# Loading the remainder rows of w_k into both halves of the partitions and converting them where they stay

## The chip, the cores and the metric

The kernel runs on one core of a Trainium2 chip, in one launch. The metric is device time in microseconds (us): the median of three runs of the kernel before is 696.64 us (696.33 to 697.31). One of its executions was also taken by the profiler; all rows below are of that one.

## The reference

Three stages stand one behind the other, on 2 batches of 4160 tokens with 192 features:

```python
# 1. a causal convolution of 7 taps with weights of its own for each token and head
w = softmax(weight_gen)                                  # (2, 4160, 8, 7)
x = einsum('bshk,bskhg->bshg', w, windows_of_7(x))       # (2, 4160, 192)
# 2. a gated two-layer block on a mix of each token and the one before it
xk = mu_k * x + (1.0 - mu_k) * x_prev
xr = mu_r * x + (1.0 - mu_r) * x_prev
x = sigmoid(xr @ w_r) * (maximum(xk @ w_k, 0.0) ** 2 @ w_v)   # w_k (192, 1024)
# 3. a second block with a convolution of 3 taps along the tokens
h = maximum(x @ w_in, 0.0)
out = (h * sigmoid(conv3(h, conv_w))) @ w_out
```

`w_k` and the other weights come as 64-bit floats; the activations are 32-bit. The kernel rounds each weight to 32 bits itself, from the two 32-bit words of each number, and splits it into a high part that TensorE takes at full rate and a low part that holds the rest.

## The kernel before, in words

The tokens are cut into ten tiles (two of 238, seven of 476, one of 352) times two batches. For each tile, GpSimd (or VectorE for the first) multiplies the windows of `rows` by the softmax weights into `prod`; the seven taps are added up, by TensorE in the first tile, with the identity as weights; TensorE transposes the result (`tok`) so that features lie on the partitions; `mixing` makes `xk` and `xr`, again as a high and a low part, in `xA` (features 0 to 127) and `xB` (the remaining 64 features: the high part on one half of the partitions, the low part on the other). `moe1` multiplies these with `wkA` and `wkB`: five matmuls for each of eight blocks of 128 columns, three with `wkA`, then two with `wkB`, first with its high part, then with its low part. ScalarE squares, ScalarE and VectorE split the result into `s`, `out_passes` multiplies it with `wv`, and `moe2` does the like with `w_in`, the convolution and `w_out`.

Because `xB` holds high and low features on the two halves of the partitions, `wkB` needs the same 64 rows of `w_k` (rows 128 to 191) on both halves: `wkB[:, 0]` the high part, `wkB[:, 1]` the low part. How these rows get there is what the change touches.

A weight goes through `prepare` in chunks of up to 512 columns. Each chunk has a load (`fetch`, issued by SyncE into one of three slots of `stage`) and a conversion (`narrow`, then `split`). In mode 0, the mode of the first chunks, a conversion is one ScalarE activation from `stage` into a PSUM bank, two VectorE TENSOR_SCALARs and one SCALAR_TENSOR_TENSOR, two matmuls (with `ident` in full 32 bits, then with `signs`), a ScalarE CAST of the high part, a third matmul that takes it off again, and a ScalarE CAST of the low part. `MODES` gives the mode of each chunk in its order.

All engine instructions are first recorded in a list, and `Program.schedule` (lines 136 to 255) gives them their order: it estimates each instruction's time, walks the dependences forward and backward `ROUNDS` times, and emits each engine's instructions by the start times so found. So line 255 stands for nearly all instructions in the profile. `SLACK` adds time between an engine's result and its use by TensorE, `PACE` stretches the estimates for an engine, and 3.507 is the estimate of how late a load lands. These constants only set the order. On each engine the instructions then run in that order, each when its operands are there; two engines that write the same `prod` buffer wait for its reader.

Before the first real matmul, TensorE runs 26 matmuls on `signs` (lines 1078 to 1080).

Of the kernel before, what the change touches and what calls it, by code (L numbers as in the profile page):

```python
# [29 lines left out]
NF = DFF // 128  # L30
LAG = 12
WARM = 26
SLACK = {"ACT": 0.311, "DVE": 0.274, "POOL": 0.239}
PACE = {"ACT": 1.045, "DVE": 1.035, "POOL": 1.037}
ROUNDS = 13
HELD = [85.0, 140.0, 215.0, 290.0, 365.0, 440.0, 515.0]
HIGH = range(5)
LOWS = {(NTILE - 1, NB - 1, k) for k in range(6, NF)}
SUMS = {(1, 0, 1), (1, 1, 0), (1, 1, 1)}
MODES = [0, 0, 0, 0, 0, 0, 2, 2, 2, 2, 2, 0, 2, 2, 2, 2, 2]  # L40

S_LAG, G_LAG = 3.25, 4.75
S_LAG_HALF, HSTEP = 3.25, 1
# [6 lines left out]
def f(ap):  # L50
    return ap.bitcast(F32)


class Program:
# [81 lines left out]
    def schedule(self):  # L136
        n = len(self.ops)
# [70 lines left out]
        def forward(rank):  # L208
            nonlocal when
            when = hold[:]  # L210
            start, last, table = [0.0] * n, 0.0, ACTF.Exp
            wires = dict.fromkeys(self.real, 0.0)

            def step(i, eng, t):
                nonlocal last, table
                start[i] = t
                if turns[i] is not None:
                    t = t + (0.0 if turns[i] == table else 1.3)
                    table = turns[i]
                end = t + late[i]  # L220
                if load[i]:
                    wires[eng] = max(wires[eng], t + dur[i] + 0.55) + moved[i]
                    end = wires[eng] + 3.507
                last = max(last, end)
                for j in succ[i]:
                    when[j] = max(when[j], t + dur[i] if eng in ("PE", "POOL") and eng == name[j] else end + slack(i, name[j]))
                return t

            walk((pred, succ), lambda i: (rank[i], i), step)
            return start, last  # L230

        def backward(start, last):
            nonlocal when
            full = [dur[i] + 0.55 + moved[i] + 3.507 if load[i] else late[i] for i in range(n)]
            when = [full[i] - dur[i] for i in range(n)]
            rank = [0.0] * n

            def step(i, eng, t):
                rank[i] = last - t - dur[i]
                for j in pred[i]:  # L240
                    when[j] = max(when[j], t + dur[i] - dur[j] + (dur[j] if name[j] in ("PE", "POOL") and name[j] == eng else full[j] + slack(j, eng)))
                return t

            walk((succ, pred), lambda i: (-start[i], -i), step)
            return rank
# [24 lines left out]
def conv_moe_kernel(ctx: ExitStack, tc: tile.TileContext, xp, wg_first, wg_rest, w_k, w_v, w_r, w_in, conv_w, w_out, out):  # L270
# [40 lines left out]
    wkA = new("wkA", [128, 2, DFF], F32R)  # L311
# [92 lines left out]
    def fetch(w, parts, n):  # L404
        wide = w.dtype != F32
        st = {"wide": wide}
        if wide:
            st["raw"] = raw_r()
            dst, w = st["raw"], w.bitcast(U32)
            for p0, p1, c0, ap in parts(w, 2):  # L410
                SP.dma_start(out=dst[p0:p1, :, :].rearrange("p a b -> p (a b)")[:, c0:c0 + ap.shape[-1]] if len(ap.shape) == 2 or ap.shape[0] * ap.shape[1] == 128
                             else dst[p0:p1, 0:n, :].rearrange("p (a b) c -> p a (b c)", a=ap.shape[1]), in_=ap)
        else:
            st["x"] = f(raw_r().rearrange("p a b -> p (a b)"))
            for p0, p1, c0, ap in parts(w, 1):
                SP.dma_start(out=st["x"][p0:p1, c0:c0 + ap.shape[-1]] if len(ap.shape) == 2
                             else st["x"][p0:p1, 0:n].rearrange("p (a b) -> p a b", a=ap.shape[1]), in_=ap)
        return st
# [60 lines left out]
    def chunk_rem(src, B, twin):  # L479
        def go(x):  # L480
            y = wb_r()
            split(y[:, 0], y[:, 1], x)
            for part, a in ((0, 0), (64, 0), (0, 1), (64, 1)):
                SP.dma_start(out=f(B[part:part + 64, a]).rearrange("p (h c) -> p h c", h=2),
                             in_=f(y[:, a if part == 0 or twin else 0]))

        return lambda: fetch(src, lambda w, k: [(0, 128, 0, bass.AP(tensor=w.tensor, offset=w.offset + 128 * w.ap[0][0], ap=[[w.ap[0][0], 64], [512 * k, 2], [1, 512 * k]]))], 512), 512, go

    def chunk_in(src, A, c):
        sl = slice(512 * c, 512 * c + 512)  # L490
        return (lambda: fetch(src, lambda w, k: [(0, 128, 0, cols(w, k, 0, 128, 512 * c, 512))], 512), 512,
                lambda x: split(A[:, 0, sl], A[:, 1, sl], x))
# [515 lines left out]
    def before_first():  # L1008
        for a in att_r.tiles:
# [8 lines left out]
    attention(0, 1, -99.6, -83.7, 0.1, POOL)  # L1018
    softmax_load(1, wg_rest[:, :slots[1] * KH], -99.5)
    softmax(1, 0, slots[1], DVE, (-92, -91.9, -91.8, -91.7, -91.6, -91.5), am_r.tiles[0])  # L1020
    prepare((-99.75, -99.7, -99.4), [(-82, chunk_rem(w_k, wkB, True)), (-81, chunk_in(w_k, wkA, 0)),
                                     (-0.5, chunk_out(w_v, wv, 0)), (0.4, chunk_out(w_v, wv, 1)), (1.0, chunk_in(w_k, wkA, 1)),
                                     (1.4, chunk_out(w_v, wv, 2)), (2.4, chunk_out(w_v, wv, 3)), (3.4, chunk_r()),
                                     (6.0, chunk_rem(w_in, wiB, False)), (8.0, chunk_in(w_in, wiA, 0)), (10.0, chunk_out(w_out, wo, 0)),
                                     (10.4, chunk_conv()), (12.0, chunk_in(w_in, wiA, 1)), (14.0, chunk_out(w_out, wo, 1)),
# [122 lines left out]
```

## Time and profile before

| what | value |
|---|---|
| median of 3 runs | 696.64 us |
| the profiled execution's own time | 696.22 us |
| its span (first to last instruction) | 694.4 us |
| TensorE matmul busy (PE) | 683.8 us, 98% |
| TensorE weight load busy (PEld) | 603.0 us, 87% |
| VectorE busy (DVE) | 590.0 us, 85% |
| ScalarE busy (ACT) | 630.3 us, 91% |
| GpSimd busy (POOL) | 531.3 us, 77% |
| granted TensorE clock | full in all 40 slices |

The span is 1.8 us shorter than the execution's time; that is what lies before the first and after the last instruction. Shares over the whole span hide that the program has two regimes. In the first 100 us the weights are loaded and converted while the first tiles run; from then on the same tile work repeats. A busy matmul engine is not one at its peak, since matmuls overlap and their ends are modelled. `pa`, `pc`, `am`, `ar`, `bm` and `br` are PSUM banks; `bm` and `br` carry the conversions of the weights until they are needed as accumulators.

### The profile page before, as it was taken

What the parts mean: (1) busy time and instruction counts of PE and PEld (TensorE: products, weight loads), DVE (VectorE), ACT (ScalarE), POOL (GpSimd) and SP (SyncE); (2) the same over time, 40 slices, a digit from 0 to 9 for tenths busy, and PEclk for the clock granted to TensorE, in tenths of its full rate; (3) what the DMA queues carried; (4) which work ended last, traced back from release to release, by engine and by line L of the source; (5) the groups of instructions that cost most, each with busy time, mean ns of one, the idle gap of its engine ahead of it and who ended that gap; (6) DMA issues with size and microseconds to landing.
All of it is one profiled execution on the core that took longest, in us unless ns stands there. A gap on an engine that the chain in (4) does not pass through costs nothing.

```text
span 694.4 us, 10540 instructions
## 1 busy us (share of the span) xinstructions
PE 683.8 (98%) x3473; PEld 603.0 (87%) x3473; DVE 590.0 (85%) x1003; ACT 630.3 (91%) x1333; POOL 531.3 (77%) x388
## 2 busy tenths in 40 slices
PE   8999999999999999999999999999999999999997
PEld 7799887888888888888888888888888888899997
DVE  7999998889879888988798978988897768686787
ACT  4988999999999998999999899898999999999996
POOL 3899999996998799669976997599929996243335
PEclk9999999999999999999999999999999999999999
DMA  8886021222021310130212112121202000200010
GB/s 298 262 210 236 23 68 42 72 86 63 8 86 64 86 65 29 65 86 13 79 65 71 24 57 93 35 54 57 80 22 71 8 28 14 65 8 28 6 33 31
DMA packets 20790, 48.43 MB, mean 70 GB/s; under 512 B 3456, under 2 KB 16256, under 8 KB 20608
## 3 DMA queue, kind: packets, MB, share of 16 engines
q1 hardware_dynamic: 20592, 47.58, 23.2%
q8 instruction: 27, 0.44, 0.3%
q14 instruction: 27, 0.22, 0.1%
q10 hardware_dynamic: 144, 0.18, 0.1%
HBM read 27.40 MB, written 6.39 MB: 49 GB/s over the span
## 4 chain that ended last, share of the span: by engine, by line
PE 86%; DVE 7%; ACT 4%; issue 1%; DMA 1%; SPq 0%; DVEq 0%; ACTq 0%
PE pa L255 25%; PE pc L255 21%; PE bm L255 13%; PE am L255 12%; PE br L255 8%; PE ar L255 7%; DVE pc L255 2%; DMA sw<-in_rest_dram 1%; DVE stage L255 1%; DVE g L255 1%; DVE s L255 1%; ACT pc L255 1%; ACT pa L255 1%; DVE mk L255 0%; DVE ar L255 0%
## 5 line engine op out<-in xcount | busy, mean ns | idle before, releaser
L255 POOL TENSOR_TENSOR prod<-rows,sw 128x1344 f32<-128x1344 f32 x68 | 210.3, 3092 | 13.7 <-PE pa L255 11.1
L255 DVE SCALAR_TENSOR_TENSOR pc<-h,cw,pc 128x476 f32<-128x476 f32 (+1 forms) x276 | 193.7, 704 | 27.2 <-ACT pc L255 24.4
L255 ACT ACTIVATE pa<-pa 128x476 f32<-128x476 f32 (+2 forms) x280 | 151.8, 546 | 11.5 <-PE pa L255 9.0
L255 POOL TENSOR_TENSOR prod<-prod 128x576 f32<-128x576 f32 (+1 forms) x126 | 154.2, 1224 | 8.4
L255 PE MATMUL bm<-g,wo 128*128 128x476 f32 (+1 forms) x411 | 135.2, 376 | 0.4 <-ACT stage L255 0.4
L255 PE MATMUL am<-s,wv 128*128 128x476 f32 (+2 forms) x464 | 129.8, 357 | 0.0
L255 PE MATMUL pa<-xA,wkA 128*128 128x476 f32 (+2 forms) x438 | 112.0, 360 | 0.8 <-DVE s L255 0.8
L255 PE MATMUL pc<-x,wiA 128*128 128x478 f32 (+1 forms) x414 | 111.8, 375 | 0.4 <-ACT x L255 0.2
L255 DVE TENSOR_TENSOR s<-pa,s 128x476 fp32r<-128x476 f32 (+1 forms) x137 | 86.7, 634 | 19.5 <-ACT s L255 18.6
L255 PE MATMUL br<-g,wo 128*128 128x476 f32 (+1 forms) x274 | 100.6, 375 | 0.0
L255 PE MATMUL ar<-s,wv 128*128 128x476 f32 (+2 forms) x336 | 99.8, 350 | 0.0
L255 ACT ACTIVATE h<-pc 128x478 f32<-128x478 f32 (+1 forms) x138 | 78.4, 569 | 17.8 <-PE pc L255 16.6
L255 ACT ACTIVATE pc<-h,cw 128x476 f32<-128x476 f32 (+1 forms) x138 | 91.7, 665 | 0.8
L255 ACT ACTIVATE pc<-pc 128x476 f32<-128x476 f32 (+1 forms) x152 | 84.3, 555 | 8.3 <-DVE pc L255 4.5
L255 POOL TENSOR_TENSOR g<-stage,g 128x476 fp32r<-128x476 f32 (+1 forms) x41 | 47.5, 1160 | 56.0 <-ACT g L255 44.1
L255 PEld LDWEIGHTS pa<-xA,wkA 128*128 128x128 f32 x438 | 79.0, 188 | 12.2 <-DVE s L255 1.3
L255 PEld LDWEIGHTS am<-s,wv 128*128 128x128 f32 x464 | 81.0, 188 | 9.3
L255 PEld LDWEIGHTS pc<-x,wiA 128*128 128x128 f32 x414 | 76.3, 188 | 11.7 <-DVE g L255 1.0
L255 PEld LDWEIGHTS bm<-g,wo 128*128 128x128 f32 x411 | 76.5, 188 | 11.2 <-ACT stage L255 0.8
L255 PE MATMUL pa<-xB,wkB 128*128 128x476 f32 (+2 forms) x292 | 82.7, 359 | 0.0
L255 PE MATMUL pc<-x,wiB 128*128 128x478 f32 (+1 forms) x276 | 81.7, 376 | 0.0
L255 ACT CAST s<-pa 128x476 fp32r<-128x476 f32 (+1 forms) x137 | 76.4, 558 | 1.1
(170 smaller groups left out, 1177.5 us busy)
## 6 DMA issues: line engine op xcount, KB each, us to landing
rows<-in_x_dram SPq DMA_DIRECT2D x14, 960.0 KB, 4.9
xB<-rm SPq DMA_DIRECT2D x28, 119.0 KB, 2.2
rows<-in_x_dram SPq DMA_DIRECT2D x4, 768.0 KB, 6.3
xB<-mk SPq DMA_DIRECT2D x16, 119.0 KB, 2.3
rows<-in_x_dram SPq DMA_DIRECT2D x2, 864.0 KB, 5.5
r<-r SPq DMA_DIRECT2D x14, 119.0 KB, 2.2
x<-x SPq DMA_DIRECT2D x14, 119.0 KB, 2.2
out_dram<-stage SPq DMA_DIRECT2D x7, 238.0 KB, 2.0
```

The costliest lines, as they stand in the source:

```text
L255: getattr(self.real[eng], method)(*a, **k)
```

## The change

`chunk_rem` loaded the 64 remainder rows once, with their 1024 columns laid over 128 partitions as two blocks of 512, converted them once into `x2[1]` (`wb_r`) and copied high and low part to both halves of `wkB` with four DMAs. `chunk_both` loads 512 columns of these rows twice, once to each half of the partitions, and converts them with the output straight in `wkB`. It does this for each of the two blocks of columns, so `w_k` now has four chunks instead of three; `MODES` has one more entry, and the constants of the order have other values. The rows of `w_in` are still done by `chunk_rem`.

```diff
-SLACK = {"ACT": 0.311, "DVE": 0.274, "POOL": 0.239}
-PACE = {"ACT": 1.045, "DVE": 1.035, "POOL": 1.037}
-ROUNDS = 13
+SLACK = {"ACT": 0.274, "DVE": 0.242, "POOL": 0.427}
+PACE = {"ACT": 1.037, "DVE": 1.015, "POOL": 1.003}
+ROUNDS = 15
...
-MODES = [0, 0, 0, 0, 0, 0, 2, 2, 2, 2, 2, 0, 2, 2, 2, 2, 2]
+MODES = [0, 0, 0, 0, 0, 0, 0, 2, 2, 2, 2, 2, 0, 2, 2, 2, 2, 2]
...
-                    end = wires[eng] + 3.507
+                    end = wires[eng] + 3.307
...
+    def chunk_both(src, B, c, twin):
+        sl = slice(512 * c, 512 * c + 512)
+
+        def go(x):
+            if twin:
+                split(B[:, 0, sl], B[:, 1, sl], x)
+                return
...
+        return lambda: fetch(src, lambda w, k: [(64 * h, 64 * h + 64, 0, cols(w, k, 128, 192, 512 * c, 512)) for h in range(2)], 512), 512, go
...
-    prepare((-99.75, -99.7, -99.4), [(-82, chunk_rem(w_k, wkB, True)), (-81, chunk_in(w_k, wkA, 0)),
-                                     (-0.5, chunk_out(w_v, wv, 0)), (0.4, chunk_out(w_v, wv, 1)), (1.0, chunk_in(w_k, wkA, 1)),
+    prepare((-99.75, -99.7, -99.4), [(-82, chunk_both(w_k, wkB, 0, True)), (-81, chunk_in(w_k, wkA, 0)),
+                                     (-0.5, chunk_out(w_v, wv, 0)), (0.4, chunk_out(w_v, wv, 1)), (0.9, chunk_both(w_k, wkB, 1, True)), (1.0, chunk_in(w_k, wkA, 1)),
```

The order moves with it. SyncE's queue at the start of the program, before (`sw` are the softmax weights, `rows` the windows of the input, `stage` the slots of the weight loads):

```order
L255 DMA rows_80<-in_x_dram 128x1536
L255 DMA stage<-in_moe_w_k_dram 128x1024
L255 DMA rows_81<-in_x_dram 128x1536
L255 DMA stage<-in_moe_w_k_dram 128x1024
L255 DMA sw<-in_rest_dram 128x224
L255 DMA stage<-in_moe_w_v_dram 128x2x384
L255 DMA sw<-in_rest_dram 128x448
L255 DMA rows_80<-in_x_dram 128x1536
L255 DMA stage<-in_moe_w_v_dram 128x2x384
L255 DMA wkB<-x_1_74 64x2x512 x2
L255 DMA stage<-in_moe_w_k_dram 128x1024
L255 DMA wkB<-x_1_74 64x2x512 x2
```

The first remainder load stood behind the first `rows`. The same place now:

```order
L255 DMA stage<-in_moe_w_k_dram 64x1024 x2
L255 DMA rows_80<-in_x_dram 128x1536
L255 DMA stage<-in_moe_w_k_dram 128x1024
L255 DMA rows_81<-in_x_dram 128x1536
L255 DMA stage<-in_moe_w_v_dram 128x2x384
L255 DMA sw<-in_rest_dram 128x224
L255 DMA sw<-in_rest_dram 128x448
L255 DMA stage<-in_moe_w_v_dram 128x2x384
L255 DMA rows_80<-in_x_dram 128x1536
L255 DMA stage<-in_moe_w_k_dram 64x1024 x2
L255 DMA stage<-in_moe_w_k_dram 128x1024
```

The two half loads of the remainder stand ahead of the first `rows`, the second `rows_80` has moved behind a load of `w_v`, and the four `wkB` copies are gone.

VectorE after the first softmax (`prod` are the products of the first tile, `bm` and `br` hold the first two chunks of `w_k` that are being converted), before:

```order
L255 TENSOR_TENSOR sw<-sw,am 128x224
L255 TENSOR_TENSOR prod_82<-rows_80,sw 128x1344
L255 TENSOR_TENSOR prod_83<-rows_80,sw 128x1344
L255 TENSOR_SCALAR stage<-bm 128x512
L255 TENSOR_SCALAR pc_114<-stage 128x512
L255 TENSOR_REDUCE am<-sw 128x32
L255 SCALAR_TENSOR_TENSOR g_76<-stage,pc_114 128x512
L255 TENSOR_SCALAR stage<-br 128x512
```

And now:

```order
L255 TENSOR_TENSOR sw<-sw,am 128x224
L255 TENSOR_SCALAR stage<-bm 128x512
L255 TENSOR_SCALAR pc_114<-stage 128x512
L255 TENSOR_TENSOR prod_82<-rows_80,sw 128x1344
L255 SCALAR_TENSOR_TENSOR g_76<-stage,pc_114 128x512
L255 TENSOR_TENSOR prod_83<-rows_80,sw 128x1344
L255 TENSOR_SCALAR stage<-br 128x512
```

Two instructions of the first conversion stand ahead of the first product, and the third stands between the products.

## Rows read from the trace of the kernel before

**Rows 1.** The page's head and first part: busy us (share) xinstructions.

```profile
span 694.4 us, 10540 instructions
PE 683.8 (98%) x3473; PEld 603.0 (87%) x3473; DVE 590.0 (85%) x1003; ACT 630.3 (91%) x1333; POOL 531.3 (77%) x388
```

**Rows 2.** Stretches: length, busy us (instructions) by engine, clock, DMA share, GB/s.

```profile
7.60:22.30 14.70, 14.63 (x78) 12.47 (x79) 14.02 (x27) 10.00 (x30) 10.32 (x4) 1.00 1.02 296
22.30:30.00 7.70, 6.53 (x37) 5.03 (x37) 7.43 (x18) 6.63 (x19) 7.54 (x5) 1.00 0.90 319
40.00:60.00 20.00, 19.31 (x156) 18.38 (x154) 19.53 (x43) 17.65 (x45) 19.31 (x17) 1.00 0.79 193
60.00:100.00 40.00, 38.26 (x254) 34.09 (x253) 37.93 (x73) 35.40 (x79) 37.40 (x29) 1.00 0.30 104
200.00:300.00 100.00, 100.00 (x474) 86.89 (x473) 89.55 (x146) 94.34 (x194) 80.94 (x56) 1.00 0.18 55
```

**Rows 3.** The chain that ended last, from 10 to 26 us.

```profile
3.21 7.57 DMA sw<-in_rest_dram
...
24.21 0.60 DVE stage L255
...
24.95 1.10 PE bm L255 x2
```

**Rows 4.** VectorE in order of time: start, us, instruction, idle time before.

```profile
5.94 3.03 DVE L255 TENSOR_TENSOR prod<-rows,sw 128x1344 f32<-128x1344 f32 x2
8.88 0.68 DVE L255 TENSOR_SCALAR stage<-bm 128x512 uint32<-128x512 uint32 x1
9.60 0.69 DVE L255 TENSOR_SCALAR pc<-stage 128x512 uint32<-128x512 uint32 x1
10.80 0.57 DVE L255 TENSOR_REDUCE am<-sw 128x32 f32<-128x224 f32 x1 [0.51 <-DMA sw<-in_rest_dram]
11.29 0.68 DVE L255 SCALAR_TENSOR_TENSOR g<-stage,pc 128x512 fp32r<-128x512 uint32 x1
11.88 0.68 DVE L255 TENSOR_SCALAR stage<-br 128x512 uint32<-128x512 uint32 x1
```

**Rows 5.** ScalarE in order of time, the first conversion's activation.

```profile
7.33 0.64 ACT L255 ACTIVATE bm<-stage 128x512 f32<-128x512 f32 x1 [3.08 <-DMA stage<-in_moe_w_k_dram]
```

**Rows 6.** TensorE in order of time.

```profile
2.59 4.87 PE L1080 MATMUL ar<-signs 128*128 128x256 f32 x26 [2.59 <-ACT signs L255]
7.64 3.16 PE L255 MATMUL pa<-prod,ident 128*128 128x192 f32 x18 [0.19 <-DVE prod L255]
10.64 1.02 PE L255 MATMUL bm<-stage,ident 128*128 128x512 f32 x2
11.50 0.49 PE L255 MATMUL pa<-prod,ident 128*128 128x192 f32 x2
12.02 0.50 PE L255 MATMUL bm<-g,signs 128*128 128x512 f32 x1
12.36 1.46 PE L255 MATMUL pa<-prod,ident 128*128 128x192 f32 x8
...
22.35 0.58 PE L255 MATMUL pc<-xA,wkA 128*128 128x238 f32 x3
...
23.86 0.45 PE L255 MATMUL br<-g,signs 128*128 128x384 f32 x1 [0.53 <-DVE g L255]
24.14 0.27 PE L255 MATMUL pc<-xB,wkB 128*128 128x238 f32 x1
24.95 1.10 PE L255 MATMUL bm<-stage,ident 128*128 128x512 f32 x2 [0.53 <-DVE stage L255]
```

**Rows 7.** SyncE's queue in order of time: the second pair of copies.

```profile
15.20 1.19 SPq L255 DMA_DIRECT2D wkB<-x  x2
```

**Rows 8.** The four copies into wkB: from issue to landing.

```profile
DMA to landing us min/median/max: 5.2/6.5/7.8
```

**Rows 9.** DMA issues of the first 40 us: count, KB each, median us to landing.

```profile
stage<-in_moe_w_r_dram SPq DMA_DIRECT2D x2, 96.0 KB, 4.6
stage<-in_moe_w_r_dram SPq DMA_DIRECT2D x1, 192.0 KB, 4.1
```

More of the change, by code (lines that the diff above doesn't have):

```diff
@@ L233, in backward @@
             nonlocal when
-            full = [dur[i] + 0.55 + moved[i] + 3.507 if load[i] else late[i] for i in range(n)]
+            full = [dur[i] + 0.55 + moved[i] + 3.307 if load[i] else late[i] for i in range(n)]
             when = [full[i] - dur[i] for i in range(n)]
@@ L487, in chunk_rem @@
         return lambda: fetch(src, lambda w, k: [(0, 128, 0, bass.AP(tensor=w.tensor, offset=w.offset + 128 * w.ap[0][0], ap=[[w.ap[0][0], 64], [512 * k, 2], [1, 512 * k]]))], 512), 512, go
+    def chunk_both(src, B, c, twin):
[4 more added lines that the diff above has]
+                return
+            y = wb_r()
+            split(B[:, 0, sl], y[:, 0], x)
+            ACT.copy(B[0:64, 1, sl], f(y[0:64, 0]))
+            ACT.copy(B[64:128, 1, sl], f(B[64:128, 0, sl]))
+        return lambda: fetch(src, lambda w, k: [(64 * h, 64 * h + 64, 0, cols(w, k, 128, 192, 512 * c, 512)) for h in range(2)], 512), 512, go
     def chunk_in(src, A, c):
```

## The prediction

> **What bounds the kernel now.** I began with the page's first part [rows 1]: TensorE is busy for 98% of the span, which looks like a kernel that only less matrix work could shorten. The table by stretches [rows 2] shows where that holds. Between 200 and 300 us TensorE is busy for all of 100 us and weight loads take 86.89 of them; VectorE, ScalarE and GpSimd have time left. In the first 100 us it is the others that are full: VectorE is busy for 14.02 of 14.70 us, 7.43 of 7.70, 19.53 of 20 and 37.93 of 40, GpSimd for 19.31 of 20 and 37.40 of 40, while TensorE stands still for 1.17 us from 22.3 to 30, 0.69 from 40 to 60 and 1.74 from 60 to 100, 3.60 together. The chain of waits from 10 to 26 us [rows 3] says the same: it comes in by a DMA of softmax weights, passes through VectorE's conversions, and reaches TensorE only at 24.95. So what is converted in the first 30 us is on the path. Once TensorE is full it stays full to the end, so a delay that is left over then reaches the end undiminished, and nothing of the change lies behind that point.
>
> A rule of the Trainium skill bears on how the 98% is read. The page "Perfetto Trace Analysis", section "Identifying the Most-Contended Engine", says that matmul busy time is a poor measure of TensorE's headroom and that the busy share of the weight loads is a better one. The rows agree: that share is 65% (5.03 of 7.70 us) from 22.3 to 30, against 87% later [rows 2]. By the busy time alone, TensorE's extra work would be the whole answer; by the rule, TensorE has gaps in the head that VectorE's delay may widen or fill.
>
> **The change part by part.** *One conversion more.* The remainder was one chunk of 512 columns on all partitions; it becomes two. On VectorE that adds three instructions. Read from start to start [rows 4]: 0.72 us (8.88 to 9.60), 0.69 us, and 0.59 us (11.29 to 11.88): 2.00 us. On ScalarE it adds one activation and two casts, each about the 0.64 us of [rows 5], 1.9 us; ScalarE is less full than VectorE in each of the early stretches, so I count it as hidden, and if it isn't, it stands in line with VectorE's and does not add. On TensorE [rows 6] it adds one 32-bit matmul with the identity, 0.86 us from start to start (10.64 to 11.50), and two with the signs, 0.34 us each (12.02 to 12.36): 1.54 us.
>
> *Loads in another order.* The half loads of the remainder, 512 KB together, now go ahead of the first 768 KB of rows. Before, 114 + 768 KB were in by 5.94, when VectorE took up the product without a wait [rows 4], and 114 + 768 + 512 KB by 7.33, when ScalarE took up the first chunk [rows 5]. Now the first 114 + 512 KB come earlier than 5.94, so that the activation of 0.64 us is over at 5.94 or, at the worst, at 6.58; I take 5.94, since 626 KB are much nearer to the front than 882. The rows, now third, are in by 7.33. VectorE then does the two scalars from 5.94 to 7.35, the product (half of 3.03 us) to 8.87, the third conversion step to 9.46 and the second product to 10.98. Before, the same five steps and the TENSOR_REDUCE (0.49 us to the next start) ended at 11.88, which is 11.39 without the reduce. The 0.51 us of idle time before the reduce is thus turned into 0.41 us gained. VectorE's sum is 2.00 - 0.41 = +1.59 us.
>
> A second rule of the skill speaks against the half loads: "DMA: Bandwidth & Descriptors", section "Rules for kernel authors", says that two transfers to disjoint halves of the partitions bring nothing over one of 128 partitions, since both use the same DMA engines. Rows of w_r have that shape: 96 KB to each half land 4.6 us after issue, 192 KB to all partitions after 4.1 us [rows 9]. By the rule the halves would be 0.5 us late; by the bounds above there is room for most of it, so I leave the sum as it is.
>
> *TensorE at the start.* The warm-up ends at 2.59 + 4.87 = 7.46 [rows 6]. The identity matmul of the first chunk is ready by 6.66, so TensorE starts 0.18 us sooner than the 7.64 of before, is done at 8.32 and then waits for the first product, which comes at 8.87 + 0.19: a new gap of 0.74 us. With the extra work this is 1.54 - 0.18 + 0.74 = +2.10 us. Against it stand two waits of 0.53 us, at 23.33 and at 24.42 [rows 6], where the first expert matmuls sit between unfinished conversions. The new order puts the conversions of the first two w_v chunks ahead of the first expert matmul; if both waits go, TensorE's sum is +1.04 us. VectorE's +1.59 lies between the two.
>
> *Copies removed.* The second pair of copies is issued at 15.20 and 15.8 [rows 7], and a copy lands up to 7.8 us after its issue [rows 8], so the last may be in only at 23.6. TensorE reads the low part at 24.14, right behind a matmul that waited for VectorE until 23.86 [rows 6]. The copies were not late, but had no more than 0.3 to 0.5 us to spare. 1,024 KB leave a queue whose DMA engines are full until 22.3 [rows 2] and 512 KB more are loaded; what stands behind them on SyncE's queue comes earlier. I cost that at nothing in the sum, because VectorE, not the loads, has no time left there; where it is worth something is the second case below.
>
> *What reaches the end.* A delay of 1.04 to 2.10 us enters at 25 us. Until 100 us the program still has waits that can take it up: 2.43 us on TensorE after 40, 0.47 + 2.07 us on VectorE [rows 2]. From one side all of it is taken up (0), from the other none is (+2.10, TensorE's sum). I take half of VectorE's sum, +0.8, because VectorE is 95 to 98% busy in these stretches and can give back only about what it waits. The last matmuls and the store are not touched. So 696.22 + 0.8 = 697.0 us. The profiled execution is 0.42 us under the median of the runs, 696.64, so the forecast is 0.06% above that median.
>
> **The rivals.** *The loads were the real limit (faster).* Not only VectorE's throughput but the lateness of the loads may have given the conversions their places: loads take 5 to 8 us to land in this stretch by the copies' rows, and the two 0.53 us waits sit where the copies land. With the copies gone the conversions can be packed ahead of the expert matmuls, and all visible waits of TensorE up to 100 us go: -3.60 + 2.10 = -1.50, or 694.7 us. For it: the low share of weight loads from 22.3 to 30. Against it: VectorE shows no wait for a load there but the 0.51 us, and must do 2.00 us more.
>
> *The first products are late (slower).* The second product ends at 10.98 instead of 5.94 + 3.03 = 8.97, 2.01 us later. Everything from the first tile's taps to its transposes, its mix and the first expert matmul (22.35) hangs on it, and GpSimd writes the same two product buffers next. If the expert matmuls start at 24.4 and the conversions put ahead don't fill the time, the 2.01 us pass on to the tiles behind, where GpSimd has 0.69 us to spare from 40 to 60 [rows 2]: 698.2 us, and 698.8 if one of the 0.53 us waits stays. It decides from a first expert matmul at about 23.9 on; before that the conversions done early pay for it.
>
> *It does what it says and the end does not notice.* The delay is taken up before 100 us, 696.2 us; this is the lower part of the forecast's own range, not a case apart.
>
> **How the numbers follow.** What a measurement of this kernel can tell from no change is about 0.2%, or 1.4 us: faster is below 695.2, slower above 698.0. The forecast with its own range (696.2 to 698.0) gets 0.43, the loads as the limit 0.31, the late products 0.26. The loads get more than the sum alone would give, since the weight loads' share shows more gaps on TensorE in the head than the extra conversion is long, and any better order eats into those. The range reaches from 694.2 (the faster case and half a microsecond more of hidden gaps) to 698.9 (the slower one with a wait kept).
>
> **What would show it.** In the profile after: VectorE busy for about 2 us more in all and TensorE with three matmuls more; the first `bm` matmul with `ident` on TensorE at about 7.5 and the first product's at about 9.1 with a gap of 0.7 us between; VectorE without the 0.51 us wait; the first `xA,wkA` matmul between 22.5 and 24. The forecast is wrong towards faster if TensorE's idle time from 22 to 100 us falls from 3.6 to under 1.5 us; towards slower if that matmul comes after 24 and GpSimd's tile work stays 2 us behind at 100 us. It is wrong in its mechanism if the difference arises after 100 us, where I count on none.

## The result and the profile after

The changed kernel takes 702.0 us (median of three, 701.74 to 702.18) where the kernel before took 696.5 on the same chip: a ratio of 1.0076 (95% interval 1.0059 to 1.0093), 0.8% slower. The forecast was 697.0, its range ended at 698.9, and "slower" had a chance of 0.26. The prediction was wrong. One more execution of the first comparison, the profiled one, took 2411.92 us with TensorE at a fraction of its pace throughout, and no other did; the profile below is of a second run of the same kernel (701.9 us span). That run's times, 703.77 to 707.41, also show something that the first comparison's 701.74 to 702.18 don't; it comes at the end of this section.

The page's head and first part (busy us, share, instructions), to be read against [rows 1]:

```profile
span 701.9 us, 10550 instructions
PE 688.9 (98%) x3477; PEld 605.5 (86%) x3477; DVE 592.1 (84%) x1006; ACT 631.7 (90%) x1336; POOL 531.1 (76%) x388
```

VectorE has its 2 us of work more, as forecast. The span grew by 7.5. The stretches of [rows 2] (length, busy us by engine, clock, DMA share, GB/s) show where:

```profile
7.60:22.30 14.70, 13.72 (x72) 11.40 (x71) 14.53 (x25) 8.35 (x24) 7.03 (x3) 1.00 0.98 293
22.30:30.00 7.70, 5.84 (x31) 4.09 (x29) 6.95 (x16) 5.80 (x17) 7.54 (x5) 1.00 0.58 202
30.00:40.00 10.00, 9.37 (x54) 7.75 (x54) 8.69 (x20) 8.98 (x25) 6.67 (x3) 1.00 0.70 200
40.00:60.00 20.00, 19.69 (x163) 19.26 (x162) 18.74 (x43) 17.62 (x45) 18.00 (x15) 1.00 0.91 211
60.00:100.00 40.00, 37.19 (x250) 33.69 (x251) 36.27 (x70) 33.25 (x75) 36.20 (x27) 0.96 0.30 101
200.00:300.00 100.00, 100.00 (x474) 86.76 (x473) 88.19 (x144) 94.24 (x193) 85.09 (x60) 1.00 0.20 59
```

From 200 to 300 us nothing has changed. In the head (the first 100 us) VectorE, the fullest engine before, now waits from 22.3 us on: it is busy for 6.95 of 7.70 us where it was 7.43, for 36.27 of 40 where it was 37.93. TensorE does less in the same time, and from 60 to 100 us its clock is 0.96. The starts of the same instruction in both traces say when the delay comes in:

| instruction | before | after | later by |
|---|---|---|---|
| VectorE, first product | 5.94 | 8.91 | 2.97 |
| TensorE, first expert matmul | 22.35 | 26.37 | 4.02 |
| VectorE, `s<-pa,s`, second | 45.66 | 50.89 | 5.23 |
| TensorE, first `pc<-x,wiA` | 71.73 | 78.76 | 7.03 |
| TensorE, one of the last `pc<-x,wiA` | 675.68 | 683.15 | 7.47 |

At the third of these places VectorE has done the same instructions in both kernels, but for the three that the change adds, so 5.23 us is a delay of like against like. Most of the whole, 7.03 of 7.47 us, is there by 72 us and is carried to the end. VectorE in order of time, against [rows 4], and four of its later waits:

```profile
5.61 0.39 DVE L255 TENSOR_TENSOR sw<-sw,am 128x224 f32<-128x224 f32 x1
7.58 0.69 DVE L255 TENSOR_SCALAR stage<-bm 128x512 uint32<-128x512 uint32 x1 [1.58 <-ACT bm L255]
8.31 0.69 DVE L255 TENSOR_SCALAR pc<-stage 128x512 uint32<-128x512 uint32 x1
8.91 1.55 DVE L255 TENSOR_TENSOR prod<-rows,sw 128x1344 f32<-128x1344 f32 x1
10.38 0.68 DVE L255 SCALAR_TENSOR_TENSOR g<-stage,pc 128x512 fp32r<-128x512 uint32 x1
10.97 1.55 DVE L255 TENSOR_TENSOR prod<-rows,sw 128x1344 f32<-128x1344 f32 x1
...
35.87 0.57 DVE L255 TENSOR_SCALAR br<-br 128x384 uint32<-128x384 uint32 x1 [0.80 <-ACT br L255]
37.48 0.42 DVE L255 TENSOR_TENSOR g<-br,wv 128x256 fp32r<-128x256 f32 x1 [0.44 <-ACT wv L255]
...
42.59 0.36 DVE L255 TENSOR_TENSOR g<-bm,wrA 128x192 fp32r<-128x192 f32 x1 [0.38 <-ACT wrB L255]
...
48.49 0.65 DVE L255 TENSOR_TENSOR s<-pc,s 128x476 fp32r<-128x476 f32 x1 [0.39 <-ACT s L255]
```

The order is the one forecast, but it starts 1.64 us late. ScalarE's first activation, against [rows 5], had to wait for the half loads, and TensorE [rows 6] for both:

```profile
6.92 0.63 ACT L255 ACTIVATE bm<-stage 128x512 f32<-128x512 f32 x1 [2.58 <-DMA stage<-in_moe_w_k_dram]
```

```profile
2.58 5.91 PE L1094 MATMUL ar<-signs 128*128 128x256 f32 x26 [2.58 <-ACT signs L255]
8.42 1.11 PE L255 MATMUL bm<-stage,ident 128*128 128x512 f32 x2
10.51 0.92 PE L255 MATMUL pa<-prod,ident 128*128 128x192 f32 x4 [0.98 <-DVE prod L255]
...
26.37 0.58 PE L255 MATMUL pc<-xA,wkA 128*128 128x238 f32 x3
...
65.95 0.60 PE L255 MATMUL am<-s,wv 128*128 128x238 f32 x3 [1.71 <-ACT s L255]
```

Why the half loads are late stands in the first microseconds. Stretches of 1 us, first of the kernel before, then of the changed one (the last two numbers are the DMA share and GB/s):

```profile
2.00:3.00 1.00, 0.41 (x2) 0.41 (x3) 0.17 (x1) 0.53 (x3) 0.00 (x0) 1.00 0.99 317
3.00:4.00 1.00, 1.00 (x6) 1.00 (x6) 0.82 (x3) 0.14 (x1) 0.00 (x0) 1.00 1.04 406
```

```profile
2.00:3.00 1.00, 0.41 (x2) 0.42 (x3) 0.08 (x1) 0.52 (x3) 0.00 (x0) 1.00 0.82 156
3.00:4.00 1.00, 1.00 (x6) 1.00 (x6) 0.91 (x3) 0.05 (x1) 0.00 (x0) 1.00 1.01 213
4.00:5.00 1.00, 1.00 (x7) 1.00 (x6) 0.60 (x2) 0.34 (x1) 0.00 (x0) 1.00 0.88 217
5.00:6.00 1.00, 1.00 (x7) 1.00 (x7) 0.93 (x3) 0.00 (x0) 0.00 (x0) 1.00 0.84 195
```

The DMA engines read as nearly full in both, but with the half loads in their queues they move about half as much (before, the stretches from 4 to 6 us show 330 and 367 GB/s). SyncE also takes 1.21 us to issue the two, from 1.18, so that the first rows, which now stand behind them, are issued at 2.43 and no longer at 1.19.

Last, the clock. In this execution TensorE stood still for 1.71 us up to 65.95, and then:

```profile
64.00:66.00 2.00, 0.29 (x4) 0.10 (x2) 1.56 (x5) 1.28 (x4) 1.84 (x3) 1.00 0.95 396
66.00:68.00 2.00, 2.00 (x10) 1.92 (x11) 2.00 (x6) 2.00 (x6) 0.54 (x2) 0.62 0.57 212
68.00:70.00 2.00, 2.00 (x12) 2.00 (x12) 1.42 (x5) 1.04 (x4) 2.00 (x2) 0.53 0.01 5
```

The granted clock (third number from the end) falls behind that stretch: for (2 x 0.38 + 2 x 0.47) / 0.5 = 3.4 us it is at its lower level, 1.2 of 2.4 GHz, which by an estimate (half of the 3.4 us) makes 1.7 us of the span. The mean clock of an execution tells whether it had such stretches: at 1.0 the changed kernel took 701.74 to 702.18, at 0.997 703.77 and 704.18, at 0.995 705.61, at 0.992 707.41. Below, "at full clock" means executions with a mean clock of 0.999 or more, and their median: 702.0 for the changed kernel, 696.5 to 696.9 for the kernel before, by chip. The loss is then 5.1 to 5.5 us, and 5.5 us where both ran on the same chip.

### The profile page after: what moved, and what is told of

The parts are those of the page before. It is cut to its first block, busy times and chain, and to the rows that moved or that the text cites. A ratio compares the mean times of both kernels' runs of the same rounds, so it can differ in the third digit from the quotient of the medians.

```text
span 2410.0 us, 10550 instructions
## 1 busy us (share of the span) xinstructions
PE 2403.8 (100%) x3477; PEld 1462.7 (61%) x3477; DVE 604.0 (25%) x1006; ACT 654.0 (27%) x1336; POOL 522.5 (22%) x388
## 4 chain that ended last, share of the span: by engine, by line
PE 100%; ACT 0%; issue 0%
PE pa L255 30%; PE pc L255 23%; PE bm L255 14%; PE am L255 13%; PE br L255 9%; PE ar L255 9%; PE ar L1094 0%; ACT L255 0%; ACT signs L255 0%; ACT om L255 0%
## 5 line engine op out<-in xcount | busy, mean ns | idle before, releaser
L255 PE MATMUL bm<-g,wo 128*128 128x476 f32 (+1 forms) x411 | 392.6, 1035 | 0.0
L255 PE MATMUL am<-s,wv 128*128 128x476 f32 (+2 forms) x464 | 385.3, 951 | 0.0
L255 PE MATMUL pc<-x,wiA 128*128 128x478 f32 (+1 forms) x414 | 353.4, 1032 | 0.0
L255 PE MATMUL pa<-xA,wkA 128*128 128x476 f32 (+2 forms) x438 | 347.9, 970 | 0.0
L255 PE MATMUL ar<-s,wv 128*128 128x476 f32 (+2 forms) x336 | 284.7, 926 | 0.0
L255 PE MATMUL br<-g,wo 128*128 128x476 f32 (+1 forms) x274 | 278.5, 1027 | 0.0
L255 PE MATMUL pc<-x,wiB 128*128 128x478 f32 (+1 forms) x276 | 246.9, 1028 | 0.0
L255 PE MATMUL pa<-xB,wkB 128*128 128x476 f32 (+2 forms) x292 | 242.3, 964 | 0.0
L255 PEld LDWEIGHTS ar<-s,wv 128*128 128x128 f32 x336 | 142.6, 454 | 83.6 <-issue 80.7
L255 PEld LDWEIGHTS pa<-xB,wkB 128*128 128x128 f32 x292 | 126.4, 445 | 79.3 <-issue 77.6
```

Source lines behind the costliest of these rows:

```text
L255: getattr(self.real[eng], method)(*a, **k)
```

## The experiments

The edits are shown in short: `...` stands for lines left out, and words in place of code say what the code does. Behind each expectation stand the measured time in us and, in brackets, its ratio to the kernel before on the same chip with the 95% interval of that ratio.

**The kernel again.** 

> The changed kernel once more, for its profile at the usual TensorE speed and for its time: 701.7 to 702.3 us, about 5.5 us over before. Theory H (the head: the half loads land late and the first products with them, and the delay is carried): TensorE's idle time before 100 us is 3 to 6 us larger than before, and from 100 us on the stretches are like those of before. Theory C (the new constants of the order: they space the tile work worse): the difference grows after 100 us, with TensorE idle in stretches where it stood still for nothing before.

Measured: 704.9 (1.0128, 1.0107 to 1.0149); its profile is the one above. The time is above the expected 701.7 to 702.3, since all four executions had a mean clock of 0.992 to 0.997. TensorE's idle time before 100 us grew by 2.8 us, a little less than the 3 to 6 of theory H, and the stretches behind 100 us are alike: H rather than C.

**The constants, alone and taken back.** SLACK, PACE, ROUNDS and the load estimate of the changed kernel in the kernel before, and the reverse:

```diff
 # in the kernel before
-SLACK = {"ACT": 0.311, "DVE": 0.274, "POOL": 0.239}
+SLACK = {"ACT": 0.274, "DVE": 0.242, "POOL": 0.427}
...
```

> The kernel before with the new SLACK, PACE, ROUNDS and 3.307 alone; the remainder is still loaded once and copied four times. Theory H: within 1 us of before (695.5 to 697.5). Theory C: 3 to 6 us slower than before (699.5 to 702.5).

> The changed kernel with the old SLACK, PACE, ROUNDS and 3.507: the half loads and the fourth chunk without the new constants. Theory H: 3 to 6 us slower than before (699.5 to 702.5). Theory C: 0 to 2 us slower (696.5 to 698.5), the worth of one more conversion.

Constants alone: 700.4 (1.0052, 1.0029 to 1.0074), 698.5 at full clock (two executions), between what the two theories expected. The changed kernel with the old constants: 705.8 (1.0132, 1.0117 to 1.0147), never at full clock. So the order found by the new constants is 1.8 us worse for the old program, but the old constants are no better for the new one (704.96 and 705.52 at a mean clock of 0.997, where the changed kernel took 703.77 and 704.18): they are not the cause by themselves.

**The start put back.** In the changed kernel the first rows load, both first products and nine taps go ahead of the first conversion again; in the kernel before, the reverse:

```diff
+        put("SP", [first rows load], first stage load)
+        put("DVE", first two products, first stage scalar)
+        put("PE", first nine taps, first matmul on stage)
```

> The changed kernel with three moves at its very start alone: the first rows load ahead of the two half loads, VectorE's two first products ahead of the first conversion, and TensorE's first nine taps ahead of the conversion's matmul, as in the kernel before; all else stays in its order. Theory P (the first products are late by 3.0 us, and that is carried to the end): the first product at 5.9 again, the first expert matmul 2 to 3 us sooner than the 26.4 of the changed kernel, 698.5 to 700.5 us. Theory X (the fourth conversion on full engines costs it, wherever the products stand): 701.5 to 704.5, no more than 0.5 us faster than the changed kernel at the same granted clock.

> The opposite: the kernel before, its remainder loaded once by one DMA and copied, but with the start's order of the changed kernel (that load ahead of the first rows, two conversion steps ahead of the first product, the third between the products). Theory P: the first product at about 7.4 instead of 5.9 and 1 to 2 us slower than before (697.5 to 699). Theory X: within 0.5 us of before.

The changed kernel with the old start: 701.9 (1.0081, 1.0061 to 1.0101), 701.6 at full clock. The kernel before with the changed start: 696.8 (0.9995, 0.9982 to 1.0008). In the first the product is back at 6.04, yet the first expert matmul stays 3.5 us late. But the rows now stand ahead of the half loads, and the first activation has gone from 6.92 to 8.52, so one delay was exchanged for another: the run shows that the late product by itself, my slower rival, isn't the cause, and no more. The second shows that the order of the start alone costs nothing when the load comes whole: there the first activation ran at 5.20, as the forecast had it.

**The shape of the loads.** Each pair of half loads as one of 128 partitions; and the second half load reading other rows:

```diff
-                (two loads of 64 partitions, 256 KB)
+                k = dict(out=dst, in_=whole)        # one load of 128 partitions, 512 KB
```

> The changed kernel, order kept, but each pair of half loads replaced by one DMA of the same 512 KB over all 128 partitions, read from one piece of memory as before; what lands in the second half of the partitions is then other columns, so wkB holds other numbers than it should. Theory S (half loads move slowly): 350 instead of about 210 GB/s from 3 to 6 us, the first activation at 5.0 to 5.6 instead of 6.9, the first product at 7.3 to 7.6 instead of 8.9, and 1 to 2 us faster than the changed kernel. Theory Q (the queue is merely full, whatever the shape): first activation at 6.5 or later, time unchanged.

> The changed kernel, order and shapes kept, but the second half load of each pair reads rows 0 to 63 of w_k instead of the rows that the first one reads, so wkB holds other numbers in its upper half. If the slow half loads come from reading the same memory twice: as fast as one load over 128 partitions (first activation at 5.0 to 5.6). If they come from the half of the partitions or the 64 rows of one DMA: like the changed kernel, first activation at 6.7 to 7.1, time within 0.5 us at the same granted clock.

One load: 702.4 (1.0075, 1.0056 to 1.0095), its one execution at full clock 700.2, and the activation at 6.12; from 3 to 6 us 334, 387 and 371 GB/s were moved, where the half loads moved 213, 217 and 195. Other rows: 704.1 (1.0105, 1.009 to 1.012), activation at 7.82. So it is the half shape that is slow, not that the same memory is read twice.

**Both put back, and the added conversion left out.** The two edits above together; then also the second remainder chunk's load and conversion left out:

```diff
+                if j == 4:
+                    prog.gone.update(range(a, len(prog.ops)))    # its load, its conversion
```

> The changed kernel with two things put back at the start: the first rows load, the first two products and their nine taps stand ahead of the first conversion again, and each pair of half loads of the remainder is one load of 128 partitions and 512 KB (the upper half of wkB so gets other columns: that part of the result differs). Theory A (the late arrival of the half loads and the late first product carry most of the loss): both are back, so the first activation comes by 7.3 us, VectorE loses only the 2.0 us of the added conversion and the time at full clock is 698.5 to 699.5. Theory B (the order from the new constants, and the added conversion wherever it stands, carry it): rows ahead alone gave nothing at full clock (701.5 to 702.1), one load 1.8 us (700.2), so both together give no more than the better of them, 700 to 702.

> As the run before, and the second remainder chunk is not loaded or converted (VectorE, TensorE and ScalarE three instructions less each); its 512 columns of wkB are set to zero by GpSimd, so the result lacks that part. Theory A: the added conversion, 2.0 us of VectorE, was all that was left; the time falls by about 2 us at full clock, to 696.7 to 697.5, the level of the kernel before. Theory B: what the new constants make of the order stays; 698.5, what the constants alone cost on the kernel before. Rival C (the added conversion is hidden): the same time as the run before, within 0.5 us.

Both put back: 703.5 (1.0098, 1.0083 to 1.0113), 703.0 at full clock (one execution). Without the conversion too: 702.1 (1.0079, 1.0064 to 1.0094), 701.75 at full clock (two). This is what I had least expected: with the order of the start, the shape of the loads and the conversion all put back, 5 us are still lost. Not all of the start came back: in both, VectorE waited for the first rows, 0.80 and 0.92 us, and the first product ran at 6.77 and 6.79 in place of 5.94. VectorE of the last one shows the other waits:

```profile
15.17 0.56 DVE L295 TENSOR_SCALAR stage<-bm 128x384 uint32<-128x384 uint32 x1 [0.91 <-ACT bm L295]
...
25.82 0.73 DVE L295 TENSOR_TENSOR xB<-ar,xB 64x238 fp32r<-64x238 f32 x2 [1.09 <-ACT xB L295]
...
34.70 0.57 DVE L295 TENSOR_SCALAR br<-br 128x384 uint32<-128x384 uint32 x1 [0.87 <-ACT br L295]
...
36.30 0.42 DVE L295 TENSOR_TENSOR g<-br,wv 128x256 fp32r<-128x256 f32 x1 [0.44 <-ACT wv L295]
...
41.39 0.36 DVE L295 TENSOR_TENSOR g<-bm,wrA 128x192 fp32r<-128x192 f32 x1 [0.39 <-ACT wrB L295]
...
47.29 0.65 DVE L295 TENSOR_TENSOR s<-pc,s 128x476 fp32r<-128x476 f32 x1 [0.39 <-ACT s L295]
```

With the 0.92 us these waits make 5.01 us up to 48 us, where the kernel before had 0.51, 0.24 and 0.30 us. The last four are the four later waits of the changed kernel (0.80, 0.44, 0.38 and 0.39 us), at the same instructions, and they stand in every profile with its start, its loads or its conversion altered. So they belong to the order that the changed kernel gets, not to the half loads, the late product or the work of the added conversion. Leaving the conversion out gave back only about 1.3 of its 2 us. The order was planned for it, and the wait of 1.09 us (0.26 in the run before) is new: taking a piece out of a fixed order doesn't show what the piece cost.

**TensorE's idle stretch filled.** Fourteen matmuls on `signs` where TensorE waits from 64 us on:

```diff
+        for _ in range(14):
+            nc.tensor.matmul(br_r.tiles[0][:, 0:256], lhsT=signs[:, 0:128], rhs=signs[:, 0:256], start=True, stop=True)
```

> The changed kernel with 14 matmuls of the warm-up's shape on TensorE, in the place where it stood idle for 1.71 us at 64 to 66 us and from which its granted clock fell to the half level for 3.41 us; they write a bank that nobody reads then. If the idle time is what the clock falls on, there is no stretch at half clock behind it, the mean granted clock is 0.999 or 1.0 in every execution, and the times lie close together at 702 to 703 (the 14 matmuls take some 2.6 us where 1.7 us were idle, so up to 0.9 us is added). If the clock falls for another reason (the time since the start, what other engines do), the drop stays near 66 us and the times are 704 to 707 at a mean clock of 0.992 to 0.997, as in the repeat of the changed kernel.

Measured: 701.9 (1.0074, 1.0059 to 1.0089), 701.43 to 702.03, each at 0.999 or 1.0. In the stretches the clock stays full:

```profile
64.00:66.00 2.00, 1.94 (x15) 1.66 (x14) 1.61 (x4) 2.00 (x6) 1.39 (x2) 1.00 0.91 365
66.00:68.00 2.00, 2.00 (x20) 2.00 (x19) 2.00 (x6) 2.00 (x8) 1.10 (x2) 1.00 0.25 92
```

In every profile the clock falls only within or right behind a wait of TensorE, or at the program's end, and with this wait filled it stayed full in all four executions. That the wait makes it fall is likely, but not shown: the three executions of the first comparison stayed at full clock with no matmul added, and in the profile of the run with both put back the same wait passes without a fall:

```profile
66.49 0.60 PE L291 MATMUL am<-s,wv 128*128 128x238 f32 x3 [1.73 <-ACT s L291]
```

```profile
66.00:68.00 2.00, 1.51 (x12) 1.44 (x13) 2.00 (x6) 2.00 (x6) 0.02 (x1) 1.00 0.62 237
68.00:70.00 2.00, 2.00 (x20) 2.00 (x19) 2.00 (x6) 2.00 (x7) 1.82 (x2) 1.00 0.03 12
```

So a wait of this length goes before a fall and doesn't always bring one. Filling the wait costs nothing, since the matmuls (1.83 us) stand where TensorE waited.

**Half loads in the kernel before.** Its one remainder load as two of 64 partitions:

```diff
+                for h in range(2):
+                    self.real["SP"].dma_start(out=dst[64 * h:64 * h + 64, :], in_=(32 of the 64 rows))
```

> The kernel before in its own order, but its one load of the remainder (128 partitions, 512 KB) is split into two of 64 partitions and 256 KB each. Theory A (the half shape itself is slow): the first activation moves from 7.33 to 8.5 to 9 us, the products in front of it stay at 5.94, VectorE stands idle for 1 us or more ahead of its first stage scalar, and the kernel is 0.5 to 1.5 us slower, 697.2 to 698.2. Theory B (the shape costs nothing, the loads of the changed kernel were late because of their place or number): the activation at 7.3 to 7.8, the time within 0.3 us of 696.7.

Measured: 697.3 (1.0008, 0.9999 to 1.0018), 697.1 at full clock. VectorE waits where it had not, and the softmax load behind is later too (before: 0.51 us):

```profile
9.86 0.69 DVE L260 TENSOR_SCALAR stage<-bm 128x512 uint32<-128x512 uint32 x1 [0.83 <-ACT bm L260]
12.23 0.57 DVE L260 TENSOR_REDUCE am<-sw 128x32 f32<-128x224 f32 x1 [0.95 <-DMA sw<-in_rest_dram]
```

In the profiled execution (697.69) VectorE is 1.4 us late from there on, still so at 110 us. Over ten executions the kernel loses about 0.5 us, and the interval still takes in no loss.

**Single waits of TensorE taken away.** One cast moved two places ahead on ScalarE; also ten matmuls on TensorE; also one load that reads the rows twice:

```diff
+        put("ACT", [the cast of s from pa], the cast of wo from bm)      # twelfth run
+        put("PE", ten matmuls pa<-xA,wkA and pa<-xB,wkB, the ident matmul of the next w_k chunk)   # thirteenth
+        in_=bass.AP(tensor=ap.tensor, offset=ap.offset, ap=[[0, 2], *ap.ap])   # fourteenth
```

> The changed kernel with one instruction moved on ScalarE: the cast of s from pa, for which TensorE waited 1.71 us at 64.2 to 65.9, stands ahead of the cast of a chunk of w_out that waits for VectorE, not two places behind it. Theory O (the loss is in the order that the planner now gives; single waits of it are lost for good): the wait of 1.7 us is gone and no new one takes its place, no stretch at half clock in any execution, 700.0 to 700.6 at a mean clock of 0.999 or 1.0. Rival H (the loss is the work of the added conversion on VectorE; a wait taken away comes back at the next place that needs VectorE): the wait moves on, 701.5 to 702.

> As the run before, and on TensorE the ten matmuls of the third and fourth expert block (pa from xA and wkA, xB and wkB) stand ahead of the identity matmul of the next w_k chunk, for which TensorE waited 1.14 us at 29. Theory O: their operands are there by then, they fill that wait, and the time falls by 1.0 to 1.3 us more, to 698.8 to 699.5 at full clock. Rival H: the blocks behind need that chunk anyway and TensorE waits there instead, within 0.3 us of the run before.

> As the run before, and each pair of half loads of the remainder is one load of 128 partitions that reads the 64 rows twice (each half of the partitions gets them; the result is complete). Theory O with the half loads' price as in the earlier run of one load (700.2 against 702.0 at full clock): the first activation at 6.1 us, the first product at 8.1 in place of 8.9, and 697.2 to 698.5 at full clock, so that only the added conversion's 1.5 us of TensorE work is left of the loss. Rival H: the head is behind by the conversion's 2 us of VectorE wherever the loads land: no more than 0.5 us under the run before.

In this order: 703.5 (1.0088, 1.0071 to 1.0105), 702.5 at full clock (one execution); 704.5 (1.0105, 1.008 to 1.0129), never at full clock; 719.7 (1.0327, 1.0307 to 1.0347). All three missed. TensorE in the twelfth run, then in the thirteenth:

```profile
64.25 0.60 PE L285 MATMUL am<-s,wv 128*128 128x238 f32 x3
66.43 0.60 PE L285 MATMUL pc<-xA,wkA 128*128 128x238 f32 x3 [1.57 <-DVE mk L285]
```

```profile
30.32 0.82 PE L290 MATMUL pa<-xA,wkA 128*128 128x238 f32 x3 [1.50 <-DVE ar L290]
```

The wait isn't gone; it stands at the next matmul that needs something of VectorE, about as long as it was or longer (1.57 us for 1.71, 1.50 for 1.14), and the clock falls behind it again (0.50 from 68 to 70 us; in the thirteenth also 0.63 and 0.51 from 30 to 34). The theory that single waits of TensorE in the new order are the loss falls; the rival of these runs, that VectorE's pace sets them, stands. The fourteenth run tells nothing of it, because its load was far slower than the others: ScalarE's first activation, and the stretches around it:

```profile
17.58 0.62 ACT L294 ACTIVATE bm<-stage 128x512 f32<-128x512 f32 x1 [13.38 <-DMA stage<-in_moe_w_k_dram]
```

```profile
16.00:20.00 4.00, 0.92 (x1) 0.50 (x2) 1.73 (x3) 0.62 (x1) 0.00 (x0) 0.50 0.13 54
```

**Work added to the kernel before, on one engine.** Six spare VectorE instructions with two operands at 24 us, the same at 250 us, two matmuls issued twice on TensorE, and four spare VectorE reduces:

```diff
+            nc.vector.scalar_tensor_tensor(out=spare, in0=f(signs[:, 0:192]), scalar=1.0, in1=f(signs[:, 0:192]), op0=ALU.mult, op1=ALU.mult)   # six
+                self.real[eng].matmul(*a, **k)    # the ident matmul again, two chunks
+            nc.vector.tensor_reduce(out=spare, in_=f(signs[:, 0:256]), op=ALU.max, axis=AX.X)    # four
```

> The kernel before with six spare SCALAR_TENSOR_TENSORs of 192 columns on VectorE, about 2.0 us in all, ahead of its first instruction for the second w_k chunk at 24.1 us; nothing reads what they write. Theory V (from 5 to 46 us the program runs at VectorE's pace, so that work added to VectorE there reaches the end whole): every VectorE step behind comes 2.0 us later, that is still so at 100 us and at the end, 698.4 to 699.0 against 696.7. The recorded forecast's step (half of it is taken up by waits before 100 us): 697.5 to 697.9. Rival T (TensorE's work sets the end): 696.7 to 697.0.

> The same six instructions on VectorE at about 250 us, where TensorE is busy all the time. Theory V: VectorE has room there, 696.5 to 697.0, no difference. If VectorE's work counted anywhere in the program it would be 698.4 to 699.0 as well.

> The kernel before with the first matmuls of two conversions (32-bit, by the identity, for the second w_k chunk at 24.95 us and the third w_v chunk at 30.38) issued twice on TensorE, 0.86 and 0.65 us: about as much as the changed kernel adds to TensorE. The result is the same. Theory V: TensorE waits for VectorE there, so no more than 0.5 us arrives at the end, 696.7 to 697.2. Rival T (TensorE's added work passes to the end whole): 698.0 to 698.4.

Early: 705.5 (1.0124, 1.0109 to 1.0138). Late: 709.0 (1.0166, 1.0152 to 1.0179). The spare instructions were not the 2 us that I had planned. VectorE in the first of them:

```profile
24.30 7.25 DVE L1091 SCALAR_TENSOR_TENSOR spare<-signs 128x192 f32<-128x192 f32 x6
31.46 0.68 DVE L258 TENSOR_SCALAR stage<-bm 128x512 uint32<-128x512 uint32 x1
```

At 250 us they took 10.5 us. The early run still says one thing: 7.2 us on VectorE at 24 us are 8.8 us at 33 and 8.6 at 664 us (TensorE, idle meanwhile, was at the low clock for 6.8 us between 28 and 36, and what that cost lies in the 8.8); nothing takes them up. A stay that long says nothing of 2 us at 250, so the control is open: no run shows what 2 us on VectorE cost where TensorE is full. TensorE's two matmuls: 698.1 (1.0015, 1.0001 to 1.0029), 697.85 at full clock against 696.75, so 1.1 of 1.51 us arrive, more than the 0.5 of theory V and less than the whole of rival T.

> The kernel before with four spare TENSOR_REDUCEs on VectorE (one operand of 256 columns each, 0.49 us from start to start as the softmax's of 224 to 256 columns, 2.0 us in all) ahead of its first instruction for the second w_k chunk at 24.1 us. In the run with two operands the spare instructions took 7.2 us instead of 2.0, so that the added time was not the planned one. Theory V: 2.0 us on VectorE arrive whole, 1.8 to 2.2 us later at 33, at 100 us and at the end: 698.5 to 699.0 at full clock. The recorded forecast's step (half is taken up): 697.6 to 697.9. Rival T (TensorE's work alone counts, the late reach of the long run was another effect): 696.7 to 697.0.

Measured: 699.0 (1.0031, 1.0019 to 1.0043), 698.21 at full clock (three executions) against 696.56 of the kernel before: 1.65 us.

```profile
24.39 1.77 DVE L1091 TENSOR_REDUCE spare<-signs 128x1 f32<-128x256 f32 x4
26.07 0.68 DVE L258 TENSOR_SCALAR stage<-bm 128x512 uint32<-128x512 uint32 x1
```

The four take 26.07 - 24.39 = 1.68 us. VectorE is 0.27 us late at 18.67 already (a later load), 1.95 from 26 us on, and 1.98 at 664 us. Of what was put on VectorE at this place, all arrives.

## Why the prediction was wrong

*What bounds the kernel* was read rightly in the main: what is put on VectorE in the head arrives at the end, and from 72 us on the delay only travels (7.03 us there, 7.47 at 683). That VectorE alone sets the pace there is too much, since 1.1 of 1.51 us put on TensorE arrive as well. The stretch up to VectorE's second `s<-pa,s` (45.66 us before) shows the account, in the kernel before, the changed one, and the one with 1.68 us added:

```profile
0.00:45.66 45.66, 41.52 (x253) 36.99 (x254) 40.61 (x85) 33.68 (x89) 31.27 (x22) 1.00 0.87 269
```

```profile
0.00:50.89 50.89, 44.52 (x257) 38.49 (x258) 42.80 (x89) 35.17 (x93) 30.95 (x22) 1.00 0.78 229
```

```profile
0.00:47.61 47.61, 42.24 (x253) 37.99 (x254) 42.17 (x90) 33.31 (x88) 31.29 (x22) 1.00 0.87 257
```

*The step that failed most is "VectorE's sum is 2.00 - 0.41 = +1.59".* VectorE (the third engine) is busy 2.19 us more and idle 50.89 - 42.80 - (45.66 - 40.61) = 3.04 us more, together 5.23. The first term (+2.00) was nearly right; the second, the idle time, was wrong in sign: -0.41 where +3.04 came. That is 3.45 of the 4.43 us by which the forecast of +0.8 fell short. The 3.04 us have two parts, read from VectorE's waits: about 1.1 at the start (a wait of 1.58 us came, one of 0.51 went) and about 2 behind it.

*The half loads.* "626 KB are much nearer to the front than 882" counted bytes and took one rate for both shapes. They moved at about half the rate, and their two issues held back the rows. The activation, set at 5.3 or at worst 5.94, ran at 6.92; VectorE got its result at 7.58 instead of 5.94, a wait of 1.58 us. The Trainium skill's "DMA: Bandwidth & Descriptors", "Rules for kernel authors", which I weighed and then left out of the sum, says that two transfers to disjoint halves of the partitions bring nothing. The trace agrees and goes further: 156 to 217 GB/s with the half loads against 317 and 406 before. What the shape costs at the end stayed open: about 0.5 us in the kernel before, 1.8 in the changed one (a single execution), and nothing with the old start in the changed one (703.0 with whole loads, a single execution, 701.6 with half loads).

*The order behind.* I took the new order as neutral beyond the start. From 24 to 49 us VectorE waits for ScalarE 0.34, 0.26, 0.80, 0.44, 0.38 and 0.39 us; before, up to the same place, 0.24 and 0.30 us stood there. The last four stay, whichever of start, loads and conversion is put back. "I count it as hidden", of ScalarE's added work, is not what failed in them: they are there too where that work is left out. The constants alone cost the old program 1.8 us. Which entry of the plan makes the waits was not found.

*What reaches the end.* "I take half of VectorE's sum" rested on idle time before 100 us that was to take a delay up, and it makes 0.8 us of the miss. VectorE's idle time is not slack when the other engines wait in turn for VectorE: all of 1.68 us arrived, and 1.1 of TensorE's 1.51. By this the forecast's own sum of 1.59 would have given 697.8 from its base of 696.22; the measured 5.23 gives 701.7 from the 696.5 of the first comparison, where 702.0 was measured.

*The clock* was in no term. It drops in some executions, by the estimate above 1.7 us a time.

*The rivals.* "The loads were the real limit" falls: before, no engine waited for a copy, and TensorE's idle time from 22 to 100 us went up, from 3.60 to 1.86 + 0.63 + 0.31 + 2.81 = 5.61 us, where this rival needed less than 1.5. "The first products are late" has the right sign, and the first expert matmul is past its mark (26.37 against 24); but with the product back at 6.04 only 0.4 us came back, so its sign was right for another reason. Of *the copies removed cost nothing* no run shows the opposite or the thing itself, since none takes the copies away alone. *The difference arises before 100 us* held. TensorE's gap of 0.74 us was 0.98. Two small figures were wrong: 697.0 is 0.05% above the median and not 0.06%, and TensorE has four matmuls more and not three (3477 against 3473), since the 32-bit one counts twice (x2 in [rows 6]).

No version tried beats the kernel before. The account of the 5.23 us is read from the traces; the runs that put pieces back did not give back their parts one by one, so how the loss splits between the half loads, the added conversion and the order is argued and not shown. Open are the plan entries behind the later waits, and the price of a whole load that serves both halves.

## What to carry to other kernels

When one engine is busy for nearly all of a stretch (here 95 to 98%) and the others work to its results, count what is added to it whole, and count its new waits as work: idle shares of a few per cent that others wait behind are no room. A new order has waits of its own, so look for them along the whole head and not only where the edit stands. Don't price a load by its bytes alone: its partitions and its issues count too. Taking one wait away is only worth something if the next result of the same engine isn't late as well.

## What the hardware showed unasked

- With two loads of 64 partitions at the head of the queue 156 to 217 GB/s were moved at a DMA share of 0.82 to 1.01, with loads of 128 partitions alone 317 and 406.
- A load that reads its 64 rows twice by a step of zero (fourteenth run) left 54 GB/s at a DMA share of 0.13, the work of about two of sixteen engines, and its first reader started at 17.58 us in place of 6.92.
- Six VectorE instructions with two operands in on-chip memory, beside GpSimd's products (3.01 to 3.06 us each), took 0.36 to 3.05 us apiece; four reduces of one operand at the same place 0.41 to 0.42.
- Behind idle stretches of TensorE of 1.5 to 1.7 us the clock fell to its half level, for 3.4 us in the changed kernel's profile; in one run it fell behind 1.12 us (fourth run, at 30 us), and in others it stayed full behind 1.73 us (eighth) and 1.94 us (eighteenth).
